# Block-sparse attention with a gated FFN: q and k loads in 2 KB runs for every block, and block transposes that write columns in token order

## The chip, the cores and the metric

The kernel runs on one core of a Trainium2 chip. The metric is device time in microseconds, and lower is better. The core has TensorE (PE) for matmuls, VectorE (DVE), ScalarE (ACT) and GpSimd (POOL) for elementwise work, SyncE (SP) whose queue issues most of the DMAs, and 16 DMA engines. PE writes its results to PSUM; everything else here lives in SBUF, which has 128 partitions.

## The reference

Four batches of eight heads, 768 tokens, 64 numbers a head. For each token an upper bound of its score against each chunk of 32 keys is formed from the least and the greatest key of the chunk; the six chunks with the highest bound are kept (and the token must not look ahead), and softmax attention runs over those. The result goes through an RMS norm and a gated FFN.

```python
k_min = np.min(k_chunks, axis=3); k_max = np.max(k_chunks, axis=3)
ub = np.sum(np.maximum(q * k_min, q * k_max), axis=-1)      # per token and chunk
top_chunks = np.argsort(where(causal, ub, -1e9))[..., -6:]
scores = where(sel & causal_token, (q @ k.T) / 8, -1e9)
x = softmax(scores) @ v                                     # 3072 tokens x 512
xn = x / sqrt(mean(x * x) + 1e-6) * rms_g
g = xn @ w_gate;  out = (g * sigmoid(g) * (xn @ w_val)) @ w_out
```

All inputs and the output are fp32.

## The kernel before

The work is cut into twelve blocks of 256 tokens, one for each batch `b` and each third `m` of its sequence. They are taken in the fixed order `ORDER`: first the four blocks with `m = 0`, then the others. A block has two groups `g` of four heads; the four heads of a group lie in four bands of 32 partitions.

**Order of work.** The kernel first records every operation (`plan.op`), with what it reads and writes and which buffers it takes. A planner ran ahead of time; its result is written out in the source: `SEQUENCE` lists the numbers of the recorded operations in the order in which they are issued, `SLOTS` gives the buffer of each tile, `CHOICE` the engine where an operation may run on several, and `WARM` the places of dummy matmuls. Each engine executes its own operations in that order and waits with semaphores for the others. So the order on each queue is fixed, and an operation that is late holds what is listed behind it on its engine.

**Loads.** `load_qk` (line 413) brings q or k of one block into `qraw` or `kraw`, a tile of 128 partitions x (group, 8, 2, 32) fp32: a partition holds eight tokens of one head. DMAs for q, k, v and the results are issued by SP (the first block's also by ACT); weights by POOL. For the first three blocks (`PACKED = {0, 1, 2}`) a partition takes eight tokens that follow one another, token = 8 r + j for partition r of the band, so a run in HBM is 8 x 64 numbers, 2 KB, and one DMA of 128 KB serves both groups of a head position: four DMAs a tile. For the other nine blocks a partition takes every 32nd token, token = 32 j + r: runs of one token, 256 bytes, and one DMA of 64 KB for each head: eight DMAs a tile. The loads of blocks 2 and 3 are held until certain weights have landed (`HELD`).

**From raw to transposed.** For each block and group, DVE transposes the raw tile in 32x32 blocks (line 621), so that the 64 numbers of a head lie on partitions (in two halves `h`) and the 256 tokens along the row: `kT`, `qT`. Four such transposes belong to a block, 48 in all. The write puts token (j, r) at place 32 j + r of the row. For the nine unpacked blocks that is token order. For the three packed blocks it is not: place 32 j + r holds token 8 r + j.

**What reads them.** `half` (lines 628 and 629) casts `kT` and `qT` to the bf16 tiles `kb` and `qb` on ACT or POOL; for packed blocks its read hops through the row so that `kb` and `qb` come out in token order. `ext` (line 636) reduces each chunk of 32 keys to its least and greatest on DVE. `relu` (line 715, on POOL or DVE) forms max(q, 0) for the bound. For blocks with `m = 0` the bound comes from matmuls at line 525 with `BO` (line 661); for the later ones from matmuls at line 507 with `BD`, which `KX` (line 466) fills, and with `QX`, a copy of `qT` in which half of the bands are exchanged by four small DMAs on SP (line 691). DVE then transposes the bounds (line 550), finds the eight highest (line 566), makes the mask (line 572) and turns it (line 576). PE computes scores (line 749) and adds the mask (line 760), ACT takes exponentials (line 799), POOL cuts the triangle (line 769), PE multiplies by v (line 825), DVE normalises (line 844). The result is scaled (line 879 or 893) and turned, for blocks 4 and up by transposing DMAs on SP (line 885), and the FFN follows (lines 949 to 1018), woven between the attention of later blocks.

Of the kernel before, what the change touches and what calls it, by code (L numbers as in the profile page):

```python
# [18 lines left out]
HUGE = 3.0e38  # L19

SEQUENCE = [
    22, 34, 37, 13, 33, 3, 35, 36, 14, 6, 38, 41, 18, 19, 4, 31, 24, 17, 29, 0, 7, 26, 39, 40, 1, 44, 48, 55,
    45, 50, 64, 56, 51, 57, 65, 46, 58, 30, 23, 12, 49, 15, 5, 62, 59, 47, 25, 28, 27, 60, 61, 42, 66, 63, 73,
    43, 20, 71, 74, 54, 67, 82, 96, 72, 16, 68, 75, 69, 145, 70, 52, 83, 97, 138, 156, 84, 146, 76, 98, 105,
    140, 106, 77, 2, 129, 107, 147, 53, 78, 108, 79, 141, 80, 21, 32, 154, 104, 86, 142, 143, 81, 150, 144, 113,
    85, 157, 87, 149, 130, 90, 88, 99, 100, 151, 101, 152, 153, 91, 89, 102, 92, 103, 114, 179, 93, 115, 131,
    109, 158, 119, 180, 8, 139, 120, 110, 132, 121, 111, 94, 159, 122, 160, 155, 123, 165, 112, 181, 116, 161,
    166, 182, 95, 1072, 164, 148, 162, 117, 118, 1073, 163, 167, 183, 124, 168, 187, 184, 173, 125, 188, 189,
    1076, 126, 213, 190, 127, 169, 191, 216, 128, 214, 133, 185, 170, 1090, 174, 175, 215, 1074, 134, 196, 217,
    1078, 1075, 1092, 218, 186, 197, 1093, 1077, 1085, 1080, 220, 198, 171, 219, 1081, 1079, 1088, 172, 223,  # L30
    202, 192, 135, 1084, 225, 1082, 203, 232, 194, 176, 193, 226, 1091, 136, 1086, 177, 204, 1102, 227, 178,
    195, 1094, 1087, 1083, 199, 1104, 205, 200, 1096, 235, 206, 1095, 234, 1098, 201, 1116, 1089, 207, 1099,
    1117, 1105, 1118, 236, 208, 230, 1103, 1120, 239, 231, 1097, 1106, 1119, 209, 237, 241, 1100, 228, 210, 229,
    238, 261, 242, 211, 224, 288, 262, 243, 221, 244, 1107, 1128, 292, 263, 264, 265, 289, 245, 1129, 240, 1130,
    222, 1134, 246, 137, 1132, 1131, 295, 233, 1140, 247, 294, 1121, 248, 293, 250, 1142, 266, 290, 1133, 1122,
    1136, 1143, 291, 251, 267, 212, 1135, 1101, 1137, 253, 296, 268, 1123, 298, 252, 1124, 300, 1138, 270, 249,
    1125, 1147, 254, 303, 271, 297, 272, 1150, 301, 1112, 273, 315, 10, 302, 269, 306, 316, 299, 1139, 1126,
    308, 364, 318, 1108, 366, 1127, 369, 317, 368, 274, 309, 365, 310, 1113, 311, 313, 370, 255, 1109, 1114,
    371, 322, 258, 1110, 372, 1141, 324, 256, 325, 259, 257, 312, 367, 319, 260, 314, 275, 278, 1144, 1111,
    1146, 320, 321, 276, 277, 374, 1145, 279, 281, 280, 326, 304, 282, 375, 1148, 1152, 373, 283, 327, 1149,  # L40
    377, 9, 328, 285, 305, 1151, 284, 329, 382, 376, 286, 330, 379, 307, 1156, 331, 287, 384, 378, 383, 332,
    450, 323, 395, 453, 333, 334, 390, 456, 345, 1161, 335, 455, 393, 457, 392, 1160, 336, 1164, 1115, 385, 337,
    454, 1172, 387, 386, 1162, 451, 397, 1153, 1174, 452, 1157, 1163, 389, 399, 458, 346, 1175, 1158, 394, 1166,
    403, 338, 1154, 396, 402, 391, 347, 339, 1173, 544, 1165, 340, 1168, 341, 400, 349, 342, 1169, 1167, 401,
    348, 1176, 343, 464, 344, 350, 1178, 468, 1170, 536, 476, 351, 1171, 465, 354, 1180, 1184, 352, 542, 355,
    353, 356, 404, 543, 357, 1191, 470, 1177, 459, 358, 1181, 1185, 462, 1186, 478, 359, 540, 1194, 1179, 1187,
    1188, 537, 361, 360, 1190, 460, 405, 1189, 481, 1182, 461, 406, 1192, 541, 1183, 388, 1193, 463, 362, 469,
    407, 398, 539, 1196, 363, 477, 1155, 408, 471, 538, 1195, 409, 380, 548, 1204, 549, 479, 1210, 551, 410,
    1206, 547, 1197, 411, 1212, 546, 1200, 473, 412, 381, 480, 483, 475, 545, 1198, 554, 485, 1205, 1213, 555,
    489, 562, 488, 414, 1208, 556, 550, 1216, 415, 472, 487, 482, 1211, 486, 417, 416, 1207, 627, 1218, 1201,  # L50
    565, 628, 1214, 413, 419, 557, 1199, 1217, 564, 632, 420, 491, 634, 1219, 1222, 490, 1220, 635, 558, 421,
    566, 428, 559, 492, 630, 1209, 567, 629, 1202, 429, 1224, 636, 418, 493, 1223, 466, 430, 561, 1225, 631,
    484, 1229, 494, 432, 568, 640, 1215, 633, 495, 1226, 425, 563, 467, 434, 1227, 1232, 642, 426, 1228, 427,
    435, 638, 496, 1235, 639, 570, 1221, 1230, 497, 433, 436, 422, 1231, 637, 431, 1234, 1238, 423, 572, 474,
    424, 498, 437, 645, 721, 1233, 440, 641, 438, 1236, 500, 439, 441, 573, 443, 1244, 442, 653, 571, 444, 574,
    1237, 501, 445, 552, 647, 499, 722, 648, 1240, 502, 503, 728, 446, 1159, 448, 654, 575, 1203, 447, 650, 576,
    505, 660, 1239, 577, 449, 506, 658, 652, 1241, 507, 578, 812, 662, 1245, 818, 504, 579, 1246, 580, 515, 665,
    649, 560, 508, 664, 516, 569, 511, 666, 509, 656, 646, 1254, 518, 663, 581, 1242, 816, 520, 510, 514, 1256,
    725, 655, 1255, 519, 521, 1257, 814, 657, 651, 1259, 512, 582, 724, 522, 667, 819, 1258, 1260, 517, 583,
    817, 513, 668, 659, 523, 713, 1261, 526, 813, 1263, 593, 524, 525, 815, 527, 529, 669, 528, 723, 1262, 530,  # L60
    553, 1265, 594, 719, 670, 531, 717, 1248, 595, 532, 726, 1249, 715, 534, 1250, 533, 585, 827, 1252, 1276,
    1251, 586, 828, 535, 671, 661, 1267, 1266, 588, 1253, 727, 1268, 1270, 584, 716, 672, 829, 720, 1277, 1272,
    587, 804, 1278, 1269, 590, 589, 718, 1273, 1295, 714, 591, 1279, 643, 837, 1289, 1297, 808, 1280, 592, 1301,
    898, 736, 839, 903, 1271, 745, 738, 1291, 806, 1298, 603, 1274, 807, 673, 596, 1304, 644, 739, 1275, 604,
    599, 902, 674, 606, 1264, 1296, 731, 905, 1292, 811, 608, 740, 597, 810, 598, 1290, 733, 609, 809, 805, 600,
    1299, 1300, 747, 1247, 734, 1317, 1302, 601, 735, 899, 676, 610, 1303, 1307, 843, 607, 741, 1319, 841, 1312,
    605, 742, 1293, 751, 1305, 732, 1320, 611, 900, 838, 840, 822, 1311, 612, 737, 748, 830, 691, 1281, 749,
    1315, 743, 824, 11, 1313, 842, 602, 744, 613, 1243, 1294, 675, 833, 1306, 890, 832, 750, 677, 1314, 1308,
    729, 1282, 1309, 678, 894, 614, 904, 825, 680, 617, 901, 1310, 826, 679, 897, 682, 835, 752, 892, 1318, 844,
    683, 618, 615, 896, 619, 753, 616, 895, 1285, 1321, 684, 681, 1283, 1316, 620, 891, 730, 831, 845, 688, 621,  # L70
    1284, 913, 834, 1286, 893, 689, 692, 836, 622, 1287, 754, 693, 690, 981, 623, 695, 846, 755, 915, 624, 697,
    756, 625, 989, 1326, 757, 698, 991, 761, 1288, 779, 746, 626, 758, 699, 1322, 922, 696, 994, 847, 694, 990,
    924, 908, 997, 759, 909, 685, 996, 1327, 848, 823, 760, 686, 849, 703, 988, 1323, 1328, 993, 762, 1324, 704,
    986, 850, 700, 763, 985, 705, 1336, 701, 995, 910, 765, 1347, 992, 911, 1338, 766, 687, 767, 707, 1329,
    1339, 912, 764, 982, 1349, 1331, 916, 925, 768, 918, 927, 1337, 702, 820, 1350, 706, 1342, 987, 851, 1334,
    821, 708, 1330, 769, 1340, 1004, 1341, 1345, 926, 709, 983, 770, 1343, 1013, 1006, 984, 1332, 1348, 919,
    928, 771, 1333, 920, 1358, 917, 1351, 1335, 772, 1353, 1344, 711, 1352, 1015, 1360, 929, 868, 1018, 780,
    921, 1346, 1354, 1019, 776, 1356, 710, 1355, 781, 1359, 999, 1357, 783, 1016, 852, 773, 998, 1014, 785,
    1361, 782, 712, 1362, 1367, 786, 930, 1007, 853, 1017, 774, 787, 775, 906, 1001, 931, 907, 1002, 1010, 859,
    932, 1020, 1325, 1368, 777, 1009, 1047, 1388, 933, 1369, 1011, 934, 784, 1382, 1390, 1021, 860, 1363, 778,  # L80
    1003, 1012, 861, 1391, 1384, 788, 935, 1385, 1022, 789, 1383, 790, 1023, 936, 1364, 794, 1024, 937, 854,
    795, 1386, 796, 791, 1365, 798, 1387, 1393, 855, 792, 793, 1025, 923, 1399, 797, 938, 857, 1389, 799, 1395,
    1372, 1396, 914, 800, 869, 1375, 1394, 802, 858, 856, 870, 801, 1392, 1401, 1377, 1397, 803, 1402, 1371,
    872, 1379, 1366, 865, 873, 1373, 944, 1398, 1374, 1378, 945, 866, 1376, 867, 1380, 862, 946, 1418, 871,
    1381, 1000, 863, 1434, 864, 1420, 1005, 1440, 1436, 874, 1437, 1442, 1421, 1413, 875, 1435, 1416, 876, 1412,
# [1019 lines left out]
```

## Time and profile before

| | |
|---|---|
| time, median of 3 runs | 306.71 us (305.89 to 307.37) |
| span of the profiled execution | 305.9 us |
| PE busy | 285.5 us, 93% |
| DVE busy | 226.8 us, 74% |
| ACT busy | 204.3 us, 67% |
| POOL busy | 162.5 us, 53% |
| DMA | 86388 packets, 35.08 MB, 74816 of the packets under 512 bytes |

The profile gives one execution; no time of that execution beside its span is on the page, and the span lies at the lowest of the three times. Busy times are shares of the span. Matmuls are pipelined and their ends are modelled, so a busy PE is not a PE at its peak. A row of the form "line engine operation out<-in xcount" stands for a group of like instructions; "idle before, <-" names what ended the idle time of the engine ahead of them. Line numbers are those of the kernel before.

### The profile page before, as it was taken

The page shows a single profiled execution, that of the slowest core. Times are in us where ns is not written, and L with a number is a line of the kernel's source. Part 1 is how long each engine was busy: PE and PEld are TensorE (multiplying, and loading weights), DVE is VectorE, ACT ScalarE, POOL GpSimd, SP SyncE. Part 2 cuts the span into 40 slices and gives each one's busy share as a digit, 9 for nine tenths or more (in the row PEclk, how much of TensorE's full clock was granted, in tenths as well). Part 3 has the DMA queues.
Part 4 walks back from the last instruction along what each step waited for, and adds up shares of the span by engine and source line. Part 5 has one row for each costly group of instructions (what it writes and reads, how often), then busy time and mean ns, then how long its engine had stood idle before and what let it go on. Part 6 is the DMA issues. An engine that isn't in the chain of part 4 may idle for free.

```text
span 305.9 us, 11386 instructions
## 1 busy us (share of the span) xinstructions
PE 285.5 (93%) x4672; PEld 217.5 (71%) x4672; DVE 226.8 (74%) x633; ACT 204.3 (67%) x353; POOL 162.5 (53%) x272
## 2 busy tenths in 40 slices
PE   7889697999999997899999996999999999999994
PEld 7567585666966865788766685678877876778763
DVE  4976979959999999679999995978545445155441
ACT  3698557457867985787987684488865776665501
POOL 4887869476964979464656443407442324214130
PEclk9999889799999999999999999899999999999999
DMA  6999999447465659456666666501103004012011
GB/s 209 208 199 198 230 181 191 86 115 162 94 163 134 153 122 173 108 130 142 158 157 132 152 153 130 133 2 27 46 2 106 2 3 105 3 71 70 2 69 69
DMA packets 86388, 35.08 MB, mean 115 GB/s; under 512 B 74816, under 2 KB 81728, under 8 KB 86336
## 3 DMA queue, kind: packets, MB, share of 16 engines
q1 hardware_dynamic: 80736, 29.12, 40.3%
q0 software_dynamic: 4752, 4.72, 9.6%
q8 instruction: 36, 0.59, 0.8%
q10 hardware_dynamic: 848, 0.53, 0.6%
q14 instruction: 16, 0.13, 0.1%
HBM read 28.58 MB, written 6.29 MB: 114 GB/s over the span
## 4 chain that ended last, share of the span: by engine, by line
PE 52%; DVE 18%; DMA 12%; SPq 6%; POOL 4%; issue 4%; ACT 2%; ACTq 0%; DVEq 0%; POOLq 0%
PE F L949 25%; PE F L996 14%; PE S L749 5%; PE F L825 5%; SPq L354 4%; DMA kraw<-in_k_dram 4%; DVE kx L636 3%; DMA QX<-qT 2%; DMA wg<-in_moe_w_gate_dram 2%; DMA qraw<-in_q_dram 2%; DVE kT L621 2%; PE S L760 2%; DVE tg L960 2%; DVE xs L879 2%; DVE m L566 2%
## 5 line engine op out<-in xcount | busy, mean ns | idle before, releaser
L799 ACT ACTIVATE pt<-S 128x1024 bf16<-128x1024 f32 (+3 forms) x104 | 86.2, 859 | 28.4 <-PE S L760 26.9
L971 POOL TENSOR_TENSOR hh<-tg,vs 128x512 bf16<-128x512 bf16 x48 | 55.8, 1168 | 41.1 <-DVE tg L960 21.4
L949 PE MATMUL F<-xsT,wg 128*128 128x256 bf16 (+1 forms) x608 | 73.4, 270 | 3.4 <-DMA wg<-in_moe_w_gate_dram 1.8
L949 PE MATMUL F<-xsT,wv 128*128 128x256 bf16 (+1 forms) x608 | 73.6, 270 | 2.5 <-DVE tg L960 2.4
L996 PE MATMUL F<-wo,hh 128*128 128x512 bf16 (+1 forms) x300 | 68.8, 373 | 1.8 <-POOL hh L971 0.6
L960 DVE SCALAR_TENSOR_TENSOR tg<-th,F 128x512 bf16<-128x512 bf16 x72 | 48.5, 678 | 27.8 <-ACT th L956 24.3
L949 PEld LDWEIGHTS <-wg 128*128 128x128 bf16 x608 | 56.2, 99 | 12.7 <-DMA wg<-in_moe_w_gate_dram 2.1
L949 PEld LDWEIGHTS <-wv 128*128 128x128 bf16 x608 | 56.3, 99 | 11.6 <-issue 2.8
L956 ACT ACTIVATE th<-F 128x512 bf16<-128x512 f32 x72 | 42.5, 599 | 24.5 <-PE F L949 23.2
L996 PEld LDWEIGHTS <-hh 128*128 128x128 bf16 x300 | 28.0, 98 | 29.0 <-issue 2.2
L769 POOL TENSOR_SCALAR_AFFINE_SELECT pt<-pt 128x512 bf16<-128x512 bf16 x48 | 31.3, 658 | 28.8 <-ACT pt L799 28.6
L825 PE MATMUL F<-VX,pt 128*128 128x65 bf16 x672 | 28.8, 195 | 7.2 <-DVE tg L960 3.0
L968 ACT ACTIVATE vs<-F 128x512 bf16<-128x512 f32 x48 | 28.6, 601 | 9.8 <-PE F L949 5.7
L825 PEld LDWEIGHTS <-pt 128*128 128x128 bf16 x672 | 26.7, 99 | 11.1 <-issue 6.7
L749 PE MATMUL S<-qb,kb 32*128 32x256 bf16 (+1 forms) x800 | 33.6, 258 | 0.1
L636 DVE TENSOR_REDUCE kx<-kT 128x16 f32<-128x512 f32 x48 | 30.7, 667 | 0.2
L964 DVE TENSOR_TENSOR hh<-tg,F 128x512 bf16<-128x512 bf16 x24 | 16.2, 677 | 12.6 <-PE F L949 12.1
L749 PEld LDWEIGHTS <-kb 32*128 32x128 bf16 x800 | 13.8, 93 | 10.4 <-issue 9.2
L760 PE MATMUL S<-mtd,chunkrow 32*128 32x128 bf16 (+2 forms) x384 | 20.6, 206 | 0.0
L844 DVE TENSOR_TENSOR xnat<-F,rden 128x256 bf16<-128x256 f32 x48 | 19.9, 419 | 1.0
L861 ACT ACTIVATE junk<-xnat 128x512 bf16<-128x512 bf16 x24 | 15.1, 631 | 8.0 <-DVE xnat L844 6.6
L760 PE MATMUL S<-mto,chunkrow 32*128 32x128 bf16 (+2 forms) x384 | 20.2, 205 | 0.1
(73 smaller groups left out, 346.7 us busy)
## 6 DMA issues: line engine op xcount, KB each, us to landing
vraw<-in_v_dram SPq DMA_DIRECT2D x24, 256.0 KB, 3.6
out_dram<-osb SPq DMA_DIRECT2D x23, 256.0 KB, 2.5
kraw<-in_k_dram SPq DMA_DIRECT2D x72, 64.0 KB, 3.0
qraw<-in_q_dram SPq DMA_DIRECT2D x72, 64.0 KB, 2.8
QX<-qT SPq DMA_DIRECT2D x32, 64.0 KB, 2.2
wg<-in_moe_w_gate_dram POOLq DMA_DIRECT2D x3, 512.0 KB, 7.4
wv<-in_moe_w_val_dram POOLq DMA_DIRECT2D x3, 512.0 KB, 8.0
wo<-in_moe_w_out_dram POOLq DMA_DIRECT2D x3, 512.0 KB, 9.6
```

Source lines behind the costliest of these rows:

```text
L636: plan.op(f"ext{n}{J}", "DVE", 0.585, 0.67, lambda n=n, op=op: VE.tensor_reduce(out=at(kx)[:, g, n], in_=at(kT).rearrange("p h (j c x) -> ...
L749: TE.matmul(s[a // 2][:, a % 2, c0:c0 + q1 - q0], kbt[r, t, ks], qbt[r, t, q0:q1], start=(t == 0), stop=(t == 1 and not mask), skip_group_ ...
L760: TE.matmul(o, chunkrow[r, BLK * kg + P * e:BLK * kg + P * (e + 1)], mv, start=False, stop=(d == 1), skip_group_check=True)
L769: GE.affine_select(out=d, in_=d, compare_op=ALU.is_ge, fill=0.0, base=0, pattern=[[0, 4], [1, P]], channel_multiplier=-1)
L799: lambda pt=pt, hs=hs, c0=c0, c1=c1, x=sc[hp]: SE.activation(out=at(pt)[:, hs, c0:c1], in_=at(x)[:, :, c0:c1], func=ACT.Exp, scale=SCALE), ...
L825: TE.matmul(o[:, a, :], p_[:, a, off:off + P], vt[:, e, a, :], start=(kb_ == 0 and a == 0), stop=(kb_ == nkb - 1 and a == 3), skip_group_c ...
L949: TE.matmul(at(p_)[:, n * W:(n + 1) * W], w[:, g, ht * P:(ht + 1) * P], at(xT)[:, g, x0:x0 + W], start=(g == 0), stop=(g == NP - 1), skip_ ...
L956: plan.op(f"tanh{U}.{hp}", "ACT", 0.48, 0.6, lambda th=th, gp=gp: SE.activation(out=at(th), in_=at(gp), func=ACT.Tanh, scale=0.5), pri - 0 ...
L960: VE.scalar_tensor_tensor(out=at(tg), in0=at(th), scalar=1.0, in1=at(gp), op0=ALU.add, op1=ALU.mult), pri - 30, reads=[th, gp], writes=[tg ...
L968: plan.op(f"vcopy{U}.{hp}", "ACT", 0.48, 0.6, lambda vs=vs, vp=vp: SE.activation(out=at(vs), in_=at(vp), func=ACT.Copy), pri + 0.1, reads= ...
L971: plan.op(f"hh{U}.{hp}", "POOL", 1.11, 1.16, lambda tg=tg, vs=vs, hh=hh: GE.tensor_tensor(out=at(hh), in0=at(tg), in1=at(vs), op=ALU.mult) ...
L996: TE.matmul(at(op)[:, cs], at(key)[:, o:o + P], wo[:, ht, cs], start=(ht == 0), stop=(ht == NHT - 1), skip_group_check=True)
```

## The change

`PACKED` goes, and all twelve blocks are loaded as the first three were: token = 8 r + j, 2 KB runs, four DMAs of 128 KB a tile. The transposes now write token (j, r) to place 8 r + j of the row, for all blocks, so that `kT` and `qT` are always in token order. The readers lose their two forms: casts, reductions, relus and the matmuls of line 525 read neighbours everywhere. `KX` no longer names `kraw` among its reads. There are 72 load operations fewer, so the operations are numbered anew in `SEQUENCE`; the order of all other operations, their engines and their dummy matmuls are as before, and each remaining load stands at the place of one that was there.

```diff
-    PACKED = {0, 1, 2}
 def load_qk(i, nm, src):
...
-            if i in PACKED:
-                sv = src[b].rearrange("(g a) (m r j) d -> a m r g (j d)", a=4, m=NBLK, r=32)[a, m]
-                todo = [(sv, lambda rows=rows: at(key)[rows].rearrange("r g j h d -> r g (j h d)"),
-                         4, 0.104 if i == 0 else 0.12)]
-            else:
-                todo = []
-                for g in range(NG):
-                    sv = src[b, 4 * g + a, BLK * m:BLK * (m + 1), :].rearrange(
-                        "(j r) d -> r j d", r=32)
-                    todo.append((sv, lambda rows=rows, g=g: at(key)[rows, g].rearrange(
-                        "r j h d -> r j (h d)"), 16, 0.019))
...
+            sv = src[b].rearrange("(g a) (m r j) d -> a m r g (j d)", a=4, m=NBLK, r=32)[a, m]
+            dma(f"load {nm}{b}{m}{a}", eng, sv,
+                lambda rows=rows: at(key)[rows].rearrange("r g j h d -> r g (j h d)"),
...
 def turn(nm):
-        lambda: VE.transpose(out=turned(nm).rearrange("p h (j r) -> p j h r", r=32, j=8),
+        lambda: VE.transpose(out=turned(nm).rearrange("p h (r j) -> p j h r", r=32, j=8),
                              in_=at(raw)[:, g]),
 def half(nm):
-            act = lambda: SE.activation(out=natural(at(hb)), in_=order(turned(nm)), func=ACT.Copy)
-            pool = lambda: GE.tensor_copy(natural(at(hb)), order(turned(nm)))
+            act = lambda: SE.activation(out=at(hb), in_=turned(nm), func=ACT.Copy)
+            pool = lambda: GE.tensor_copy(at(hb), turned(nm))
...
 # ext0, ext1
-                out=at(kx)[:, g, n], in_=at(kT).rearrange("p h (j c x) -> p h c j x", j=8, x=4)
-                if packed else at(kT).rearrange("p h (c t) -> p h c t", t=CH),
-                axis=AXXY if packed else AXX, op=op)
+                out=at(kx)[:, g, n], in_=at(kT).rearrange("p h (c t) -> p h c t", t=CH),
+                axis=AXX, op=op)
...
 # KX
-                    reads=[kx_, bd, kraw] + [kx_ + (x, "d") for x in range(NG)]
+                    reads=[kx_, bd] + [kx_ + (x, "d") for x in range(NG)]
```

More of the change, by code (lines that the diff above doesn't have):

```diff
@@ L415, in load_qk @@
         key = (nm + "raw", b, m)
-        first = True
         for n, a in enumerate((0, 2, 1, 3)):
@@ L419, in load_qk @@
             rows = slice(32 * a, 32 * (a + 1))
-            if i in PACKED:
-                sv = src[b].rearrange("(g a) (m r j) d -> a m r g (j d)", a=4, m=NBLK, r=32)[a, m]
-                todo = [(sv, lambda rows=rows: at(key)[rows].rearrange("r g j h d -> r g (j h d)"),
-                         4, 0.104 if i == 0 else 0.12)]
-            else:
-                todo = []
-                for g in range(NG):
-                    sv = src[b, 4 * g + a, BLK * m:BLK * (m + 1), :].rearrange(
-                        "(j r) d -> r j d", r=32)
-                    todo.append((sv, lambda rows=rows, g=g: at(key)[rows, g].rearrange(
-                        "r j h d -> r j (h d)"), 16, 0.019))
-            for k_, (sv, dst, packets, cost) in enumerate(todo):
-                dma(f"load {nm}{b}{m}{a}{k_}", eng, sv, dst, packets, cost,
-                    loads_due(i, nm == "q"), writes=[key],
-                    takes=[(key, nm + "raw")] if first else (),
-                    behind=[HELD[i][0]] if i in HELD and first else ())
-                first = False
+            sv = src[b].rearrange("(g a) (m r j) d -> a m r g (j d)", a=4, m=NBLK, r=32)[a, m]
+            dma(f"load {nm}{b}{m}{a}", eng, sv,
+                lambda rows=rows: at(key)[rows].rearrange("r g j h d -> r g (j h d)"),
+                4, 0.104 if i == 0 else 0.12, loads_due(i, nm == "q"), writes=[key],
+                takes=[(key, nm + "raw")] if not n else (),
+                behind=[HELD[i][0]] if i in HELD and not n else ())
     def loads_due(i, n):
@@ L627, in half @@
             T, hb = kT if nm == "k" else qT, (nm + "b", *J)
-            act = lambda: SE.activation(out=natural(at(hb)), in_=order(turned(nm)), func=ACT.Copy)
-            pool = lambda: GE.tensor_copy(natural(at(hb)), order(turned(nm)))
-            flex(f"half {nm}{J}", {"ACT": (1.0, 1.1, act), "POOL": (1.02, 1.06, pool)} if packed else {"ACT": (0.54, 0.63, act), "POOL": (0.57, 0.61, pool)},
+            act = lambda: SE.activation(out=at(hb), in_=turned(nm), func=ACT.Copy)
+            pool = lambda: GE.tensor_copy(at(hb), turned(nm))
+            flex(f"half {nm}{J}", {"ACT": (0.54, 0.63, act), "POOL": (0.57, 0.61, pool)},
                  base + 2 - first, reads=[T, T + (g,)], writes=[hb], takes=[(hb, nm + "b")])
@@ L636, in job @@
             plan.op(f"ext{n}{J}", "DVE", 0.585, 0.67, lambda n=n, op=op: VE.tensor_reduce(
-                out=at(kx)[:, g, n], in_=at(kT).rearrange("p h (j c x) -> p h c j x", j=8, x=4)
-                if packed else at(kT).rearrange("p h (c t) -> p h c t", t=CH),
-                axis=AXXY if packed else AXX, op=op), base + 1, reads=[kT, kT + (g,)] + ([kx] if n or g else []), writes=[kx + (g, n)],
+                out=at(kx)[:, g, n], in_=at(kT).rearrange("p h (c t) -> p h c t", t=CH),
+                axis=AXX, op=op), base + 1, reads=[kT, kT + (g,)] + ([kx] if n or g else []), writes=[kx + (g, n)],
                 takes=[(kx, "kx")] if not n and not g else ())
@@ L656, in job @@
             plan.op(f"KX({b}, {m_})", "DVE", 0.95, 1.0, lambda kx_=kx_, m_=m_: place(kx_, m_), base + (2 if m_ else -3),
-                    reads=[kx_, bd, kraw] + [kx_ + (x, "d") for x in range(NG)], writes=[bd, bd + (m_,)])
+                    reads=[kx_, bd] + [kx_ + (x, "d") for x in range(NG)], writes=[bd, bd + (m_,)])
         bo = ("BO", *J)
@@ L709, in go @@
             def go():
-                o, x = qr(), at(qx if m else qT)[:, g]
-                if packed:
-                    o, x = o.rearrange("p h (r j) -> p h r j", j=8), order(x)[:, :, 32 - w // 8:]
-                else:
-                    x = x[:, :, BLK - w:]
-                eng.tensor_scalar(out=o, in0=x, scalar1=HUGE, scalar2=0.0, op0=ALU.min, op1=ALU.max)
+                eng.tensor_scalar(out=qr(), in0=at(qx if m else qT)[:, g, :, BLK - w:], scalar1=HUGE, scalar2=0.0, op0=ALU.min, op1=ALU.max)
             return go
@@ L719, in job @@
         yield
-        flex(f"relu{J}", {"POOL": (0.58 if m else 0.36 if packed else 0.25, 0.62 if m else 0.4 if packed else 0.29, relu(GE)),
+        flex(f"relu{J}", {"POOL": (0.58 if m else 0.25, 0.62 if m else 0.29, relu(GE)),
                           "DVE": (0.34 if m else 0.14, 0.42 if m else 0.22, relu(VE))},
```

17 lines of the change are left out of this document (4 added, 13 removed), and 212 rows, old and new, of tables (SEQUENCE, SLOTS).

## The prediction

> **What bounds the kernel now.** I read the page first: the busy shares and the 40 slices.
>
> ```profile
> span 305.9 us, 11386 instructions
> PE 285.5 (93%) x4672; PEld 217.5 (71%) x4672; DVE 226.8 (74%) x633; ACT 204.3 (67%) x353; POOL 162.5 (53%) x272
> DVE  4976979959999999679999995978545445155441
> ```
>
> DVE's 74% is a mean over two kinds of stage: its row of slices (7.65 us each) is close to full from slice 2 to slice 25, about 190 us, and half empty after that. So I asked for the busy time of the engines in four stretches cut at those places. The columns are the stretch and its length, then PE, PEld, DVE, ACT and POOL busy us with instruction counts, the granted clock, the DMA share and GB/s.
>
> ```profile
> 5.00:17.00 12.00, 10.57 (x224) 7.89 (x222) 11.83 (x36) 7.20 (x14) 9.48 (x31) 1.00 0.96 225
> 17.00:50.00 33.00, 29.49 (x516) 23.88 (x516) 26.79 (x73) 23.38 (x50) 25.37 (x38) 0.95 1.06 199
> 50.00:190.00 140.00, 130.22 (x2276) 98.02 (x2274) 125.87 (x375) 104.18 (x179) 88.36 (x137) 0.99 0.62 138
> 190.00:306.00 116.00, 111.95 (x1636) 84.50 (x1634) 61.27 (x149) 68.10 (x110) 37.75 (x51) 0.99 0.18 49
> ```
>
> From 5 to 17 us DVE has 0.2 us to spare. From 17 to 50 us the DMA engines are full (share 1.06) and DVE has 6.2 us. From 50 to 190 us DVE is busy 125.9 of 140 us, so 14.1 us are idle, and the DMA engines stand at 0.62. After 190 us PE has the work and DVE is half idle. PE's busy time counts pipelined matmuls, so its 130 of 140 us is not a second proof of a bound. What ends DVE's idle time between 50 and 190 us is short:
>
> ```profile
> DVE rden L840 <- PE F L825: 3.4, 3, 1.5
> DVE qraw L715 <- DMA QX<-qT: 3.1, 1, 3.1
> DVE tg L960 <- ACT th L956: 2.8, 4, 1.1
> ```
>
> Then the chain of waits, piece by piece (start, length, what). Early on it runs through DVE, POOL and the weight DMAs; before 158.5 us it runs through three load issues in SP's queue, and from 160 us through DVE again.
>
> ```profile
> 10.97 0.67 DVE kT L621
> 16.45 0.31 POOL BO L661
> 16.76 0.62 POOL pt L769
> 17.69 7.36 DMA wg<-in_moe_w_gate_dram
> ...
> 30.25 0.72 DVE kT L621
> ...
> 31.68 0.62 DVE kT L621
> ...
> 43.88 1.02 POOL kb L629
> ...
> 46.02 1.01 POOL qb L629
> ...
> 156.86 0.60 SPq L354
> 157.50 0.45 SPq L354
> 158.00 0.45 SPq L354
> 158.49 2.00 DMA kraw<-in_k_dram
> 160.49 1.15 DVE qraw L715
> 161.64 0.62 DVE qT L621
> ```
>
> **The change, part by part.** *The 48 block transposes (line 621).* Their number, order and 128x512 fp32 size stay. For all 48 the write changes: each partition wrote 32 neighbouring words per 32x32 block, and now writes one word in every eighth, 32 bytes apart. Where they stand, and what one takes (min/median/max ns):
>
> ```profile
> 5.00:17.00 12.00, 5.40 (x8) 1.00 0.96 225
> 17.00:50.00 33.00, 2.71 (x4) 0.95 1.06 199
> 50.00:190.00 140.00, 23.08 (x35) 0.99 0.62 138
> 190.00:306.00 116.00, 1.16 (x2) 0.99 0.18 49
> L621 DVE STREAM_TRANSPOSE kT<-kraw x24: 664/701/712, 5.1 to 192.8; 128x512 f32<-128x512 f32 x24
> ```
>
> (One transpose lies across a cut and is counted twice.) The trace has no strided SBUF write by DVE. The nearest rows are strided reads: in the first three blocks the bf16 casts of q and k, on ACT or on POOL, read single fp32 words 128 bytes apart; in the other nine the same casts of the same 128x512 read neighbours.
>
> ```profile
> 6.40 1.10 ACT L628 ACTIVATE kb<-kT 128x512 bf16<-128x512 f32 x1 [2.22 <-DVE kT L621]
> 58.88 0.63 ACT L628 ACTIVATE kb<-kT 128x512 bf16<-128x512 f32 x1
> L629 POOL CAST kb<-kT x14: 604/612/1083, 5.8 to 226.5; 128x512 bf16<-128x512 f32 x14
> 1.73 0.37 DVE L390 TENSOR_REDUCE pat<-ident 128x32 bf16<-128x128 bf16 x1 [1.73 <-POOL ident masks.py:199]
> 2.02 0.28 DVE L384 TENSOR_REDUCE own<-ident 128x2 f32<-128x128 bf16 x1
> L636 DVE TENSOR_REDUCE kx<-kT x48: 642/674/687, 6.3 to 197.1; 128x16 f32<-128x512 f32 x48
> ```
>
> One word at a time costs 1.10 against 0.63 us on ACT and 1.083 against 0.612 us on POOL: 0.47 us more in both, 0.92 ns a word. DVE's two reductions of the same 128x128 input differ by 0.09 us: line 390 reads every element 64 bytes from the last, line 384 reads runs of 32; that is 0.7 ns an element, in a pair that is not equal otherwise. Where DVE reads runs of four neighbours (line 636 in the first three blocks) nothing is lost: the row spans only 642 to 687 ns over both layouts. [...] I take 0.47, because two engines of different make give the same price and the DVE pair points the same way. That is 48 x 0.47 = 22.6 us more DVE work, and the transpose would measure 0.70 + 0.47 = 1.17 us.
>
> [...]
>
> Where the 22.6 us fall. From 5 to 17 us eight transposes add 3.8 us to a DVE that has 0.2 us left; BO, the triangle and the wg issue at 17.69 us stand behind them, so up to 3.8 us are on the path. The DMA engines are full there and drain while the issue is late, so part comes back: I take 3 us, bounds 0 and 3.8. From 17 to 50 us four more add 1.9 us, two of them on the chain (30.25 and 31.68 us). From 50 to 190 us about 35 add 16.4 us. The two after 190 us stand where PE has the work: nothing, and 0.9 us if that cover were gone.
>
> *The casts of the first three blocks.* Twelve casts (q and k, two groups, three blocks) lose the 0.47 us each, 5.6 us off ACT and POOL together; POOL's casts at 43.88 and 46.02 us are on the chain, so 0.9 us of it counts and cancels the two transposes there. The six relus of 128x128 shorten too. ACT and POOL have slack behind DVE elsewhere, so the rest counts nothing; without that cover it would be a gain of 4.7 us. The two reductions at line 636 read neighbours now and did not suffer before: nothing.
>
> *The loads.* Nine blocks go from eight DMAs of 64 KB in 256-byte runs to four of 128 KB in 2 KB runs, for q and for k: 144 issues become 72.
>
> ```profile
> kraw<-in_k_dram SPq DMA_DIRECT2D x72, 64.0 KB, 3.0
> kraw<-in_k_dram SPq DMA_DIRECT2D x10, 128.0 KB, 3.2
> L354 SPq DMA_DIRECT2D kraw<-in_k_dram x82: 311/449/1657, 0.8 to 182.9; - x82
> L621 DVEq EVENT_SEMAPHORE  x64: 21/50/1153, 4.9 to 192.2; - x64
> SPq L885 <- DVE xs L879: 42.9, 3, 18.6
> ```
>
> At 0.45 us an issue SP's queue loses 72 x 0.45 = 32 us of work, and a load of twice the size lands in about the same time (3.2 against 3.0 us), so the last piece of a block's k or q arrives earlier, and the QX copies and the transposing DMAs queued behind the loads are issued earlier. The remaining pieces keep their places in SP's order. But SP is not starved: it waits 42.9 us for DVE's xs, and a late xs holds the loads queued behind that DMA. What an early load can give is DVE's wait for DMA, 3.1 us between 50 and 190 us, and less where the next term is DVE itself. On DVE's own queue there are fewer semaphores to wait for: 64 events of 0.05 us now; by the built order some 28 go, 1.4 us.
>
> *The rest.* The matmuls of line 525 read and write neighbours, which they partly did before; their number stays. KX no longer names kraw: the buffer comes free earlier, but the order of the loads in SP's queue is written out and unchanged, so nothing moves.
>
> **The sum.** 50 to 190 us: DVE work 125.9 + 16.4 - 1.4 = 140.9 us, already more than the 140 us of the stretch. The smallest growth, with no idle time left, is +0.9 us; with all 14.1 us of idle time kept it is +15.0 us. I take half the idle time, 7 us, because 3.1 us of it was a DMA wait and the waits for PE and ACT shrink when DVE is later: +8 us. With +3 from the start and 0 from 17 to 50 us, the span grows by 11 us to 316.9 us. The profiled span is 305.9 us, and the median of the shown runs is 306.71, 0.8 us more; that is kept, so 317.7 us. After 190 us everything shifts as it is, PE being busy without a gap that could take it up.
>
> **The rivals.** *The strided write is free.* Then the loads decide: the chain holds three load issues in a row before 158.5 us and like runs elsewhere; I give 3.1 us for the DMA wait and 1.4 us for the semaphores, less what DVE's next wait takes back: about 3.5 us, so 303.2 us. For it: no row shows a DVE write of this kind, and line 636 shows that DVE is not sensitive to layout as such. Against: ACT, POOL and the reductions. It decides from where a transpose costs less than 0.1 us extra (48 x 0.1 = 4.8 us, mostly taken up).
>
> *The full price.* DVE's idle time is not taken up, because what ends it is PE and ACT work that itself waits for DVE: all 47 transposes before the PE stage count, 22.1 us, so about 328.8 us. For it: 5 to 17 us, where there is no slack. Against: 14.1 us of idle time.
>
> *The late arrivals hide it.* DVE absorbs everything but 1 us, near 307 us. Against: 140.9 us of work in 140.
>
> **How the numbers follow.** Half a per cent, 1.5 us, is about what a measurement of this kernel can tell from no change. Forecast, between 309 and 325 us: 0.65. Full price: 0.16. Hidden, within 0.5%: 0.06. Free write, faster: 0.13. Slower is 0.65 + 0.16 = 0.81. The range goes from 304.5 (part of the free-write case) to 330 us (the full price with a little over), and leaves out about 0.16.
>
> **What would show it.** Line 621's transposes (line 594 then) at about 1.17 us and DVE busy near 226.8 + 22.6 = 249 us: if they stay at 0.70 us, the forecast falls with its main term. The casts at 0.61 to 0.66 us in all blocks; 92 instead of 164 load issues of q and k on SP, and 36864 packets of 256 bytes replaced by 4608 of 2 KB; DVE's wait for QX gone, and DVE without gaps from 50 to about 200 us. If the transposes are long and the time still does not grow, the idle time took it up. If DVE shows new waits for the raw loads, the larger DMAs land too late.

## The result: 2.6% slower, and what the profile after shows

| | before | after |
|---|---|---|
| time, median of 4 runs | 306.3 us (304.65 to 307.37) | 314.38 us (313.1 to 314.56) |
| ratio | | 1.0257, 95% interval 1.0203 to 1.0312 |
| span of the profiled execution | 305.9 us | 312.8 us |
| DMA packets | 86388 | 52979 |

The changed kernel is slower, by 8.1 us in the medians and by 6.9 us in the two profiled spans; the forecast was 11 us. Ratios here and below leave disturbed runs out, so they need not be the quotient of two medians. The profiled execution of the changed kernel took 314.49 us, 1.7 us more than its span. First the page of the changed kernel: shares of busy time, the DVE slices and the granted clock.

```profile
span 312.8 us, 11250 instructions
PE 284.9 (91%) x4640; PEld 217.9 (70%) x4672; DVE 237.9 (76%) x633; ACT 201.3 (64%) x353; POOL 160.5 (51%) x272
DVE  4965996598999999989999999997644445145441
PEclk9968996999999999999999999999999999999999
DMA packets 52979, 35.07 MB, mean 112 GB/s; under 512 B 36800, under 2 KB 43712, under 8 KB 52928
```

DVE's full slices now reach to slice 27. Line numbers in views of another kernel are its own: the transposes of line 621 stand at 594 in the changed kernel. DVE's order of instructions is the same in both kernels, so the two traces can be cut at the same four DVE instructions, those that stand nearest to 5, 17, 50 and 190 us before. The columns are those of the prediction: stretch and length, busy us of PE, PEld, DVE, ACT and POOL with counts, clock, DMA share and GB/s. Before:

```profile
5.06:17.11 12.05, 10.51 (x223) 7.83 (x222) 11.94 (x36) 7.31 (x14) 9.59 (x31) 1.00 0.96 224
17.11:52.96 35.85, 30.75 (x527) 24.89 (x527) 29.64 (x73) 25.63 (x53) 28.21 (x42) 0.95 1.07 199
52.96:190.47 137.51, 129.43 (x2270) 97.48 (x2270) 123.36 (x376) 101.82 (x175) 85.87 (x132) 0.99 0.61 137
190.47:305.90 115.43, 111.48 (x1627) 84.03 (x1624) 60.81 (x148) 68.10 (x110) 37.28 (x51) 0.99 0.18 49
```

And after:

```profile
4.98:19.47 14.49, 10.39 (x222) 7.57 (x221) 14.38 (x36) 5.88 (x14) 8.38 (x31) 0.97 1.05 197
19.47:57.84 38.37, 32.29 (x505) 25.61 (x508) 26.64 (x73) 21.07 (x49) 24.78 (x39) 0.84 1.08 204
57.84:198.05 140.21, 130.55 (x2300) 98.44 (x2313) 134.85 (x374) 104.70 (x180) 88.81 (x135) 1.00 0.50 127
198.05:312.80 114.75, 108.46 (x1601) 83.03 (x1604) 61.04 (x148) 68.21 (x110) 36.92 (x51) 1.00 0.18 50
```

The 6.9 us come as +2.4, +2.5 and +2.7 us in the first three stretches and -0.7 us in the last. In the third, DVE's busy time grows by 11.5 us (123.36 to 134.85), its idle time falls from 14.15 to 5.36 us, and the stretch grows by the difference. So more than three quarters of the new DVE work there is paid out of idle time. What DVE waited for has changed with it; in the changed kernel, from 54 to 197 us, the longest groups are

```profile
DVE tg L927 <- ACT th L923: 4.8, 4, 2.6
DVE ubn L531 <- ACT junk L828: 1.0, 1, 1.0
```

The 3.4 us for PE's F and the 3.1 us for the DMA into QX are gone. The price itself stands in the groups of the transposes (busy us, mean ns; 0.69 us before):

```profile
L594 DVE STREAM_TRANSPOSE kT<-kraw 128x512 f32<-128x512 f32 x24 | 25.7, 1099 | 2.3 <-DMA kraw<-in_k_dram 2.2
L594 DVE STREAM_TRANSPOSE qT<-qraw 128x512 f32<-128x512 f32 x24 | 25.4, 1096 | 0.0
```

That is 0.40 us more in the row. But a row is not the time that DVE gives to an instruction. In the timeline (start, length) before, and then after, the instruction behind a transpose starts while the row of the transpose still runs:

```profile
161.56 0.70 DVE L621 STREAM_TRANSPOSE qT<-qraw 128x512 f32<-128x512 f32 x1
162.19 0.14 DVE L840 RECIPROCAL rden<-F 128x4 f32<-128x4 f32 x1
```

```profile
170.64 1.10 DVE L594 STREAM_TRANSPOSE qT<-qraw 128x512 f32<-128x512 f32 x1
171.60 0.15 DVE L807 RECIPROCAL rden<-F 128x4 f32<-128x4 f32 x1
```

From start to next start it is 0.63 us before and 0.96 us after. Over all 48 transposes the median of that distance goes from 0.625 to 0.946 us: the price in DVE's time is 0.32 us, and 48 x 0.32 = 15.4 us. Those 11.5 us of the third stretch are 35 x 0.33. The whole difference of 0.08 us between 0.40 and 0.32 is the part of the longer row that lies under the next instruction.

### The profile page after: what moved, and what is told of

It is laid out like the page before. It is cut to its first block, busy times and chain, and to the rows that moved or that the text cites. A ratio compares the mean times of both kernels' runs of the same rounds, so it can differ in the third digit from the quotient of the medians.

```text
span 312.8 us, 11250 instructions
## 1 busy us (share of the span) xinstructions
PE 284.9 (91%) x4640; PEld 217.9 (70%) x4672; DVE 237.9 (76%) x633; ACT 201.3 (64%) x353; POOL 160.5 (51%) x272
## 2 busy tenths in 40 slices
DMA packets 52979, 35.07 MB, mean 112 GB/s; under 512 B 36800, under 2 KB 43712, under 8 KB 52928
## 4 chain that ended last, share of the span: by engine, by line
PE 48%; DVE 33%; issue 6%; DMA 5%; ACT 4%; SPq 1%; POOL 1%; DVEq 0%; ACTq 0%; POOLq 0%
PE F L916 24%; PE F L963 12%; DVE kT L594 6%; DVE kx L609 5%; DVE qT L594 4%; PE F L792 4%; DVE tg L927 4%; PE S L716 4%; DVE xs L846 2%; DVE BD L451 2%; DMA kraw<-in_k_dram 2%; DVE xnat L811 2%; PE S L727 1%; DMA vraw<-in_v_dram 1%; PE F L1039 1%
## 5 line engine op out<-in xcount | busy, mean ns | idle before, releaser
L963 PE MATMUL F<-wo,hh 128*128 128x512 bf16 (+1 forms) x273 | 64.9, 370 | 4.3 <-DVE tg L927 1.1
L935 ACT ACTIVATE vs<-F 128x512 bf16<-128x512 f32 x48 | 28.5, 598 | 11.1 <-PE F L916 5.7
L594 DVE STREAM_TRANSPOSE kT<-kraw 128x512 f32<-128x512 f32 x24 | 25.7, 1099 | 2.3 <-DMA kraw<-in_k_dram 2.2
L594 DVE STREAM_TRANSPOSE qT<-qraw 128x512 f32<-128x512 f32 x24 | 25.4, 1096 | 0.0
```

The costliest lines, as they stand in the source:

```text
L594: lambda: VE.transpose(out=turned(nm).rearrange("p h (r j) -> p j h r", r=32, j=8), in_=at(raw)[:, g]),
L935: plan.op(f"vcopy{U}.{hp}", "ACT", 0.48, 0.6, lambda vs=vs, vp=vp: SE.activation(out=at(vs), in_=at(vp), func=ACT.Copy), pri + 0.1, reads= ...
L963: TE.matmul(at(op)[:, cs], at(key)[:, o:o + P], wo[:, ht, cs], start=(ht == 0), stop=(ht == NHT - 1), skip_group_check=True)
```

## The experiments

Two theories stood against each other after the result. The first: the hop of the write costs about 0.4 us a transpose, most of it is hidden, and the loads give nearly nothing. The second: the write costs a good deal more on the path than 8 us, and the new loads give part of it back. A third possibility was that something else, such as PE's clock, makes part of the loss.

**The new loads without the hop.** The changed kernel, with the old write:

```diff
-VE.transpose(out=turned(nm).rearrange("p h (r j) -> p j h r", r=32, j=8), in_=at(raw)[:, g])
+VE.transpose(out=turned(nm).rearrange("p h (j r) -> p j h r", r=32, j=8), in_=at(raw)[:, g])
```

> The changed kernel, with the transposes writing neighbours again (place 32 j + r) and everything else as changed. The token order inside a block is then wrong for all readers, which still read neighbours: this leaves the reordering out, and the time is read for the write alone. Theory P (the hopping write is the price): transposes back at 0.70 us, 48 x 0.40 = 19 us less DVE work, DVE's 3.1 us wait for QX still gone, so 302 to 304 us, below the 306.3 us of before. Theory L (the larger loads and what they shift cost the time): 310 us or more, near the 314.4 us of the changed kernel.

Measured: 300.65 us (299.47 to 300.66), ratio to the kernel before, which took 307.19 us beside it, 0.9775 (0.9737 to 0.9814); that is below the 302 to 304 us of theory P. The transposes, and then the same four stretches:

```profile
L594 DVE STREAM_TRANSPOSE kT<-kraw 128x512 f32<-128x512 f32 x24 | 16.3, 693 | 2.5 <-DMA kraw<-in_k_dram 2.5
```

```profile
5.25:18.21 12.96, 10.90 (x221) 7.91 (x220) 12.36 (x37) 5.89 (x14) 8.38 (x31) 0.93 1.13 208
18.21:52.61 34.40, 29.66 (x508) 23.46 (x508) 26.23 (x74) 21.08 (x49) 24.34 (x39) 0.93 1.10 205
52.61:184.28 131.67, 128.64 (x2286) 97.22 (x2284) 122.16 (x375) 104.48 (x180) 89.20 (x136) 1.00 0.58 141
184.28:299.00 114.72, 110.42 (x1636) 83.74 (x1632) 60.78 (x148) 68.41 (x111) 37.42 (x51) 1.00 0.19 51
```

Alone, everything but the hop makes the kernel 6.5 us faster. In the two profiled spans it is 6.9 us, and 5.8 us of them lie in the third stretch (137.51 to 131.67). Between this kernel and the changed one only the write differs, and that is 13.8 us of span (299.0 to 312.8): 8.5 us in the third stretch, 4.0 in the second, 1.5 in the first. DVE's busy time in the whole execution goes from 222.6 to 237.9 us, which is 15.3 us or 48 x 0.32.

**The hop without the new loads.** The kernel before, with the new write for all blocks and nothing else.

```diff
-VE.transpose(out=turned(nm).rearrange("p h (j r) -> p j h r", r=32, j=8), in_=at(raw)[:, g])
+VE.transpose(out=turned(nm).rearrange("p h (r j) -> p j h r", r=32, j=8), in_=at(raw)[:, g])
```

> The kernel before, with its loads and its readers as they are, and only the write of the 48 transposes changed to one word in eight. The token order is then wrong, as this leaves the fitting loads out. Theory P: transposes at 1.10 us, no relief from the loads, so the 8.1 us of the change plus about 3 us: 316 to 319 us. Theory L: within 2 us of 306.3 us.

Measured: 315.12 us (313.71 to 315.68), ratio 1.0252 (1.0212 to 1.0293), a little under the 316 to 319 us of theory P and far from theory L. Its third stretch:

```profile
56.97:199.24 142.27, 131.88 (x2289) 97.93 (x2292) 135.64 (x376) 101.89 (x175) 86.46 (x132) 0.99 0.57 132
```

The ratio is that of the changed kernel (1.0257). So the same loads that are worth 6.5 us where the write is near are worth nothing that can be measured where it hops, and the same hop costs 8 us on the old loads and 13.8 us on the new. The two kernels that hop end the third stretch with nearly the same DVE busy time (135.6 and 134.9 us) and the least idle time (6.6 and 5.4 us, against 14.15 before and 9.5 without the hop). The times show that the two effects do not add. The idle times say why, as far as single traces can: the gain of the loads and the absorption of the hop draw on the same idle time of DVE, and it is spent once.

**Which part of the loads.** The kernel with the near write and 2 KB runs, but still eight DMAs of 64 KB for a block's q or k in nine blocks (its core, against the changed kernel):

```diff
+                for g in range(NG):
+                    sv = src[b, 4 * g + a, BLK * m:BLK * (m + 1), :].rearrange("(r j) d -> r (j d)", r=32)
+                    todo.append((sv, lambda rows=rows, g=g: at(key)[rows, g].rearrange(
+                        "r j h d -> r (j h d)"), 16, 0.019))
```

> As the first of these runs (neighbouring writes, wrong token order), but the loads of blocks 3 to 11 stay eight DMAs of 64 KB, now each with 2 KB runs. It parts the two halves of the new loads. If the relief comes from SP's fewer issues, DVE's wait for QX near 184 us is back and the time is about 306 us; if it comes from the longer runs, 302 to 304 us.

Measured: 303.03 us (301.83 to 304.14), ratio 0.9865 (0.9819 to 0.991). The load issues:

```profile
kraw<-in_k_dram SPq DMA_DIRECT2D x72, 64.0 KB, 2.5
qraw<-in_q_dram SPq DMA_DIRECT2D x72, 64.0 KB, 2.5
```

DVE's wait for QX is not back, and the time is that of the longer runs. The interval lies just above that of four DMAs (0.9737 to 0.9814): the 72 issues fewer are worth 2.4 us in the medians, and the long runs, together with the readers that no longer hop, the other 4.2 us. Those two were not taken apart here. (The 4.2 us are read against the 307.19 us of the kernel before.)

**Where a hop begins to cost.** A kernel that computes nothing of the reference: one kind of 128x512 fp32 instruction after the other, eight of each. Lines 37 to 47 are transposes whose write steps 1, 2, 4, 8, 16 and 32 words; 53, 55 and 57 a DVE copy (a multiplication by one) that is near, hops 8 words in its write, hops in its read; 60 to 64 the same on ACT, 68 to 72 on POOL.

```diff
+    for _ in range(N): VE.transpose(out=d.rearrange("p (b r) -> p b r", r=32), in_=x)
+    for _ in range(N): VE.transpose(out=by(2), in_=blocks(2))   # by(4), by(8) follow
```

> No attention and no FFN: only groups of eight 128x512 fp32 operations that differ in the distance of their words. Transposes on DVE writing neighbours, then every 2nd, 4th, 8th, 16th and 32nd word; a plain DVE, ACT and POOL copy with near, with hopping (every 8th word) write and with hopping read. [...] If a hopping write is a price of the transpose alone, the plain copy shows none.

Measured, as groups of lines (busy us, mean ns):

```profile
L62 ACT ACTIVATE dst<-src 128x512 f32<-128x512 f32 x8 | 9.1, 1132 | 0.3
...
L41 DVE STREAM_TRANSPOSE dst<-src 128x512 f32<-128x512 f32 x8 | 8.8, 1100 | 0.3
L70 POOL COPY dst<-src 128x512 f32<-128x512 f32 x8 | 8.8, 1099 | 0.5
L43 DVE STREAM_TRANSPOSE dst<-src 128x512 f32<-128x512 f32 x8 | 8.8, 1098 | 0.3
...
L39 DVE STREAM_TRANSPOSE dst<-src 128x512 f32<-128x512 f32 x8 | 5.7, 713 | 0.3
L37 DVE STREAM_TRANSPOSE dst<-src 128x512 f32<-128x512 f32 x8 | 5.7, 712 | 0.3
L60 ACT ACTIVATE dst<-src 128x512 f32<-128x512 f32 x8 | 5.0, 630 | 0.2
L55 DVE TENSOR_SCALAR dst<-src 128x512 f32<-128x512 f32 x8 | 5.0, 627 | 0.3
...
L53 DVE TENSOR_SCALAR dst<-src 128x512 f32<-128x512 f32 x8 | 3.4, 427 | 0.3
```

A write to every second word, 8 bytes apart, costs a transpose nothing (713 against 712 ns). To every fourth word, 16 bytes apart, it costs the full 0.39 us, and 32 bytes cost no more. On ACT and POOL the write hop costs 0.50 and 0.48 us (POOL's near copy, line 68, takes 616 ns). Here each transpose overwrites the tile of the one ahead of it, and no row lies under the next: from start to start it is about 0.75 us near and 1.13 us at 8 words, so the whole 0.39 us of the row is paid. The 0.32 us belong to the order of instructions in this kernel.

**The hop on other engines.** The changed kernel's loads and the near write, with the token order restored as the kernel before does it in its first three blocks, now in all: casts on ACT and POOL read hopping, and the matmuls of line 507 and the relus take the order into their views.

```diff
+    PACKED = set(range(len(ORDER)))
-            act = lambda: SE.activation(out=at(hb), in_=turned(nm), func=ACT.Copy)
-            pool = lambda: GE.tensor_copy(at(hb), turned(nm))
+            act = lambda: SE.activation(out=natural(at(hb)), in_=order(turned(nm)), func=ACT.Copy)
+            pool = lambda: GE.tensor_copy(natural(at(hb)), order(turned(nm)))
```

> All loads as in the changed kernel (2 KB runs, four DMAs of 128 KB), the transposes write neighbours, and the hop goes to the readers in all twelve blocks: the 48 casts on ACT and POOL read every 32nd word (1.10 and 1.08 us instead of 0.63 and 0.61), the matmuls of line 507 read QX and its relu in hops. The output is complete. DVE keeps 0.70 us a transpose. If the price matters because DVE is the bound and ACT and POOL have slack, most of the 6.5 us that the run with neighbouring writes showed is kept: 301 to 305 us. If the casts stand on the path on ACT and POOL as well (36 x 0.47 = 17 us more work there), 306 to 314 us.

Measured: 309.94 us (309.2 to 311.47), ratio 1.0143 (1.0059 to 1.0226). The third stretch, and the casts:

```profile
53.75:191.51 137.76, 133.68 (x2245) 99.32 (x2257) 124.18 (x375) 105.57 (x175) 96.44 (x132) 0.99 0.53 132
```

```profile
L615 POOL CAST qb<-qT 128x512 bf16<-128x512 f32 x17 | 18.2, 1078 | 3.9 <-DVE qT L607 3.5 <-PE S L735 0.4
L614 ACT ACTIVATE kb<-kT 128x512 bf16<-128x512 f32 x10 | 11.1, 1111 | 2.3 <-DVE kT L607 2.3
```

This is 4.4 us better than the changed kernel, but 9.3 us behind the near write without any hop (in the medians and in the spans, 308.3 against 299.0 us). Two things got longer on the way. The first is the matmuls of line 507 (493 in this kernel, 492 in the near-write one), whose operand is now read in hops. Their PE and PEld busy time in the third stretch, with the hop and then without it:

```profile
53.75:191.51 137.76, 12.15 (x384) 8.13 (x384) 0.99 0.53 132
52.61:184.28 131.67, 6.92 (x384) 5.29 (x384) 1.00 0.58 141
```

That is 5.2 us more of PE in a stretch that grew by 6.1 us and in which PE is busy 133.7 of 137.8 us; in the last stretch it is 1.75 us more (4.06 against 2.31). So 7.0 of the 9.3 us appear as busy time of these matmuls. The second is the casts. POOL stands idle for 41 us of the third stretch, and yet eight of the hopping casts on POOL and ACT stand on the chain that ended last: at 0.47 us each that is 3.8 us at most, an estimate. PE itself hardly waited for them: the waits that the profile puts down to POOL's casts are 1.2 us of ACT and 0.4 us of PEld. No run hops the casts alone, so the shares of the 9.3 us stay open; the larger part points at PE, not at ACT and POOL.

**PE's clock.** In the changed kernel the clock granted to PE falls early on. Windows of before, then after, then of the changed kernel with 20 more dummy matmuls:

```profile
20.00:22.00 2.00, 1.49 (x29) 1.19 (x29) 1.84 (x11) 2.00 (x4) 1.63 (x3) 1.00 1.20 199
50.00:55.00 5.00, 2.56 (x28) 2.31 (x26) 4.91 (x7) 2.36 (x4) 2.96 (x5) 0.85 1.12 197
```

```profile
18.00:20.00 2.00, 0.45 (x10) 0.42 (x8) 1.93 (x12) 0.83 (x3) 1.57 (x5) 0.62 1.19 211
20.00:22.00 2.00, 2.00 (x69) 1.74 (x67) 0.38 (x4) 1.86 (x5) 1.92 (x5) 0.50 1.20 195
...
50.00:55.00 5.00, 5.00 (x53) 3.83 (x50) 2.59 (x15) 0.88 (x2) 1.19 (x2) 0.50 1.07 217
```

```diff
-    (58, 86, 0, 0), (72, 4, 2, 1), (97, 10, 0, 1), (140, 6, 2, 1), (166, 2, 3, 1), (174, 5, 2, 1), (183, 1, 1,
-    1), (267, 1, 3, 1), (333, 1, 0, 1)]
+    (58, 86, 0, 0), (72, 4, 2, 1), (97, 14, 0, 1), (124, 8, 3, 1), (140, 6, 2, 1), (166, 2, 3, 1), (174, 5, 2, 1), (183, 1, 1,
+    1), (267, 1, 3, 1), (270, 8, 0, 1), (333, 1, 0, 1)]
```

> The changed kernel with 20 more dummy matmuls in three places where PE waits for DVE early on (4 more ahead of the second scores, 8 ahead of a product with v near 18 us, 8 ahead of the bound of the third block near 48 us). Theory C (part of the loss is PE's clock, granted 0.50 to 0.68 from 18 to 26 us in the changed kernel and 1.00 before): the clock stays at 1.0 there and 2 to 4 us come back at 28 us; the end moves by less, 311 to 313.5 us, if DVE takes up the rest later. Theory P alone: the delay at 28 us and the end stay within 1 us of the changed kernel.

```profile
20.00:22.00 2.00, 1.78 (x5) 0.66 (x5) 0.55 (x3) 1.24 (x3) 1.92 (x5) 0.50 1.15 176
22.00:24.00 2.00, 2.00 (x68) 1.37 (x69) 0.78 (x5) 0.23 (x1) 0.91 (x2) 0.87 1.22 199
...
50.00:55.00 5.00, 5.00 (x96) 3.99 (x95) 3.52 (x17) 1.52 (x3) 2.60 (x4) 1.00 1.02 227
```

Measured: 313.18 us (312.1 to 313.98), ratio 1.024 (1.0157 to 1.0323); span 312.1 against 312.8 us. The clock from 50 to 55 us is whole again and the early dip is shorter, the second stretch is 1.6 us shorter (36.75 against 38.37 us), and the end comes 0.7 us earlier in the spans and 1.2 us in the medians, within the scatter of both. The clock from 20 to 22 us stayed at 0.50, so theory C's repair came about in part only, and this run alone does not bound the clock. The kernel with the near write does. It has the same low clock early on:

```profile
18.00:20.00 2.00, 1.66 (x60) 1.52 (x59) 1.03 (x5) 1.58 (x5) 1.99 (x5) 0.50 1.21 197
20.00:22.00 2.00, 2.00 (x28) 1.05 (x25) 0.68 (x5) 1.60 (x4) 1.92 (x3) 0.50 1.24 202
```

It is the fastest of the kernels that do the whole work, at 300.65 us. And the hop on the old loads has a mean clock of 0.94 from 19.87 to 56.97 us, where the kernel before has 0.95 in the same stretch and the changed kernel 0.84, and is as slow as the changed kernel. So the low clock is there without the loss, and the loss without the lower clock of the stretch: the clock is not the cause.

**A hop that costs nothing.** The kernel before with 512-byte runs for its nine unpacked blocks: a partition takes two tokens that follow one another, and the write goes to every second word. Eight DMAs as before, order of tokens as the reference wants it.

```diff
-                        "(j r) d -> r j d", r=32)
+                        "(q r y) d -> r q (y d)", r=32, y=2)
...
+                        VE.transpose(out=turned(nm).rearrange("p h (q r y) -> p q y h r", r=32, y=2),
+                                     in_=at(raw)[:, g].rearrange("p (q y) h r -> p q y h r", y=2))],
```

> The kernel before with a middle way for blocks 3 to 11: a partition takes runs of two tokens (512 bytes in HBM, still eight DMAs of 64 KB), and the transposes write every second word, which in the run that varied the distance cost 0.712 us, as much as neighbours. Token order and output are complete; blocks 0 to 2 are as before. If the price begins only beyond 8 bytes in this kernel too: transposes of 0.70 us, packets of 256 bytes halved, and 303 to 306 us (the longer runs with eight DMAs gave 303.0 us without the hopping casts of the first three blocks). If a write at every second word costs after all: 1.1 us a transpose and 312 us or more.

Measured: 305.4 us, ratio 0.9936 (0.9875 to 0.9997). The interval ends too near to 1 to rest on, so the same kernel was measured again, with more executions:

> The kernel of the pairs again, unchanged, with more rounds, since its first interval against the kernel before ends just below 1. Theory (price of the far write is the whole loss; runs of 512 B keep part of the gain of longer runs): 303 to 306 us, ratio 0.985 to 0.998, transposes at 0.69 us. Rival (the first difference was chance): ratio 0.998 to 1.005.

Measured: 306.19 us, ratio 1.0009 (0.9967 to 1.0052). The first difference did not come back; the two kernels are equal within half a per cent. The transposes keep their price (18 of 24 for each of q and k take the new write):

```profile
L623 DVE STREAM_TRANSPOSE kT<-kraw 128x512 f32<-128x512 f32 x18 | 12.2, 692 | 0.0
```

So the free write is there, and doubling the run to 512 bytes buys nothing that can be measured. The two profiled executions of this one kernel also show how far a single trace may be pressed: spans 302.4 and 302.2 us, but 135.7 and 131.9 us in the third stretch, the difference made up in the first two. A difference of 2 or 3 us of one stretch between two executions is therefore weak by itself; the changes of DVE's busy time (123.2 and 122.5 us in that stretch) are firm.

## Why the prediction was right, and which of its terms were off

The direction and the mechanism held: the hopping write costs DVE, it costs more than the loads give, and part is taken up by idle time. The time was 314.38 us, 3.3 us under the forecast and inside its own case (309 to 325 us). Term by term, with the reserve that the pairs showed: a difference of 2 or 3 us of one stretch is weak.

- **The price of a transpose, +0.47 us.** Its sign and order of size were rightly taken from the hopping casts on ACT and POOL. It was mis-sized: 0.40 us in the row and 0.32 us in DVE's time. The term 48 x 0.47 = 22.6 us is 15.4 us. About half of that error, 3.4 us, is the price of another engine (0.47 for 0.40 us). The other 3.8 us are the use of a row's length as the engine's time: rows that follow one another on DVE overlap, by 0.07 us before and 0.14 us after in the two pairs of rows above, and 0.08 us more of the longer row lie under the next instruction (medians). Single words 8 bytes apart cost a transpose nothing (713 against 712 ns); no run here has a copy with that step.
- **5 to 17 us, +3 us.** It is +2.4 us, eight transposes by 0.30, with 0.1 us of idle time on DVE before and after (12.05 - 11.94 and 14.49 - 14.38), as said.
- **17 to 50 us, nothing.** It is +2.5 us between the two profiles (35.85 to 38.37). The prediction cancelled two shorter casts against two transposes of the chain and gave the other two nothing. The runs split it otherwise: everything but the hop takes 1.45 us off the stretch (35.85 to 34.40), and the hop puts 4.0 us on it with the new loads (34.40 to 38.37) and 1.25 us with the old ones (35.85 to 37.10). Four transposes of 0.32 us are 1.3 us. So all four count, where two were let go; the other 2.7 us, with the new loads only, are waiting whose cause stays open. The run with more dummy matmuls had 1.6 us less in this stretch, which a single trace does not settle.
- **50 to 190 us, +8 us.** It is +2.7 us. Two sizes were off, both to the same side: new DVE work of 11.5 instead of 15 us (the price again), and 5.4 us of idle time kept instead of 7. The rule behind it, that what DVE waits for shrinks when DVE is later, held (14.15 to 5.4 us of idle time).
- **After 190 us, nothing.** It is -0.7 us: covered by PE (busy 108.5 of 114.75 us), as said.
- **DVE busy near 249 us, transposes at 1.17 us.** They are 237.9 and 1.10 us. DVE gained 11.1 us where 22.6 were forecast. Of the 11.5 us between them 7.2 are the price. The other 4.3 us seem to be no work at all: before, one 128x64 instruction at 48.37 us (line 572) filled 4.67 us in the record, where the shortest of its line takes 0.22 us. POOL ran without a gap meanwhile, three instructions of 1.1 us from 47.85 us on and three of 0.6 us up to 52.96 us, and the row ended at 53.04 us. In the changed kernel no instruction of that line is longer than 1.43 us; in the kernel before with the hop one of 4.69 us is there again. The profile names no wait for it; by its length such a row seems to hold one, and what it waits for was not tested.
- **The loads, at most 3.1 us, with the semaphores 3.5 us where the write is free.** Mis-sized: 6.5 us where the write is near, of which 2.4 us go with the fewer issues. The gain was looked for only where DVE waits for DMA; in the near-write kernel DVE's wait for PE's F in the third stretch is 0.7 us too, where it was 3.4 us. Whether the earlier q and k or the shorter casts did that was not taken apart. Two smaller readings were off: 20 semaphore events of the transposes went, not 28 (64 to 44), and the larger loads land later, at 3.7 and 3.5 us for k and q against 3.0 and 2.8 us. The prediction compared those of k alone. In the changed kernel itself the forecast of next to nothing is right (315.12 us with the old loads, 314.38 us with the new), for the reason given: DVE is the next term. The wait for QX went, as foreseen.

The sum came nearer than its terms, and that much is luck: the price and the idle time that stays were both taken too high for the middle (+8 us for 2.7), and the second stretch too low (nothing for 2.5). The span was joined to the time by 0.8 us; the execution of the changed kernel has 1.7 us outside its span, so against its own time the forecast of the span (316.9 against 312.8 us) is off by 4.1 us, which is the fairer measure of the steps.

The rival of the free write had the right sign for its case: without the hop the time is 300.65 us, where 303.2 us had been worked out. The full price, 328.8 us, fell on 9 us of idle time taken up in the third stretch. That the late arrivals hide everything fell with the third stretch too: 134.85 us of DVE work would not fit in its old 137.5 us with the 5.4 us of idle time that stay.

## What to carry to other kernels

Before a layout is turned inside an on-chip write, look at the distance between words that follow one another: here 8 bytes were free (713 against 712 ns) and 16 bytes cost 55% of a transpose (1100 ns). Moving the hop to the readers was no free way out here: casts on ACT and POOL paid about as much for it (about 0.47 us each, against 0.40 us in the transpose's row), the matmuls that read in hops paid too (12.15 against 6.92 us of PE), and 9.3 us stayed. Price an instruction by the distance from its start to the next start in a stretch without gaps, among the neighbours that it has in the kernel, and not by the length of its row. And two effects that live on the same idle time do not add: the loads were worth 6.5 us alone and nothing beside the hop, so measure each alone and both together.

## What the hardware showed that was not expected

- The price of a hop was a step here, not a slope: 712, 713, 1100, 1098, 1033 and 1041 ns for a transpose whose write steps 1, 2, 4, 8, 16 and 32 words. The step lies between 8 bytes (713 ns) and 16 bytes (1100 ns); what makes it lie there, no run shows.
- A DVE copy of 128x512 fp32 takes 427 ns near and 627 ns with a write that hops 8 words (622 ns with such a read). The 0.20 us are half of what the transpose pays, so one engine has no one price for a hop.
- Matmuls lose with a hop too: 384 of line 507 with an operand of 64x128 fp32 read in hops took 12.15 us of PE, and 6.92 us without.
- In the changed kernel PE stood still for 1.55 us before 19.61 us, waiting for DVE, and from 20 to 22 us the granted clock was 0.50 although PE was busy all the time; before, it was 1.00 there. But the near-write kernel has 0.50 there as well and ends 13.8 us earlier: a low clock early on need not reach the end.
